# Gated mix of attention and MLP on one core: k and v summed in four column tiles, the gate's dot product on VectorE

## The chip, the cores and the metric

The kernel runs on one NeuronCore of one Trainium2 chip. The metric is the device time of one execution in microseconds (us); the time before is the median of three runs, 1220.77 us (1220.49 to 1221.15). PE is the matmul engine, PEld its weight loads, DVE the vector engine, ACT the scalar engine, POOL GpSimd, SP the queue from which most transfers are issued.

## The reference

One sequence of S = 2048 rows and width D = 512, all float32. An attention with 32 query heads of 16 elements and one shared key and value head, and an MLP with squared ReLU (width 1792), are mixed row by row with a scalar gate.

```python
def _A_ref(x, wq, wk, wv, wo):
    q = (x @ wq).reshape(B, S, H, Dh).transpose(0, 2, 1, 3)
    k = x @ wk
    v = x @ wv
    scores = jnp.einsum("bhqd,bkd->bhqk", q, k) * (Dh ** -0.5)
    p = _softmax(scores, axis=-1)
    o = jnp.einsum("bhqk,bkd->bhqd", p, v)
    return o.transpose(0, 2, 1, 3).reshape(B, S, H * Dh) @ wo

def _B_ref(x, w1, b1, w2, b2):
    h = jnp.maximum(jnp.einsum("bsd,df->bsf", x, w1) + b1, 0)
    return jnp.einsum("bsf,fd->bsd", h * h, w2) + b2

g = _sigmoid((x * gate_w).sum(-1, keepdims=True))
return g * _A_ref(x, wq, wk, wv, wo) + (1 - g) * _B_ref(x, w1, b1, w2, b2)
```

## The kernel before

**Two stages.** A short start, up to about 25 us, loads x, makes k and v for all 2048 rows and the first query tile, and sets up an upper bound of the scores. Then one long loop runs to the end. It goes over 32 query tiles (`it`: a column chunk `c` of 512 rows and a group of four heads), and for each over 32 units (128 keys by 256 queries by 4 heads). For every unit PE makes the scores (L757), ACT takes the exponential from PSUM to SBUF (L794), and PE sums e times v (L808, four heads in four column tiles of 32). Between the score matmuls of a unit, PE is given the matmuls of all other work (L1105): the remaining query tiles, the two MLP layers, the output projection. These stand in 64-row halves, so that each runs beside a score matmul of the other half. A unit of that other work is a *span*; `spans` counts them.

**What sets the order.** All instructions are issued by hand, engine by engine, in the order of the Python text (`manual_schedule`). In the loop a small planner decides: it keeps estimates of when PE, ACT and DVE are free (`at_pe`, `at_act`, `at_dve`), `PLANS` says where scores stand in a phase, and about a third of the score halves do not go straight to ACT: DVE copies them first (`score_copy`, L778, tile `x` to `e`), so that PSUM comes free earlier. DVE's other work waits in lists (`soon`, `divisions`, `chores`) with a price each; `spend` takes from them what, by these prices, fits ahead of such a copy, which may come `LATE` = 0.3 us after its scores. Entries of `chores` are strictly first in, first out; a load in that list returns how long its data is held back (`LANDS`, `DIVIDES`).

**The start.** `wkvf` holds wk, wv and gate_w as 33 used columns of 64, for four row tiles of D. For each chunk c of 512 rows, `kv_half` makes four float32 matmuls: row tiles 0 and 2 add up in the lower 64 partitions of a PSUM bank, 1 and 3 in the upper 64, in two column tiles. `kv_copy` (ACT) takes the bank to SBUF, `k_rows` (PE) adds the two halves and repeats k over the partitions with a constant matrix (`C_REP`), `k_square` and `k_round` (ACT) and `k_parts` (DVE) make k's two parts, and `k_norm` (a matmul on PE and a maximum on DVE) the largest norm of a key. After the four norms `km` and `k_shift` write a row of `k_aug`, without which no score can be made. `v_tiles` takes v and the gate's sum to rows with another constant matrix (`C_SEL`, 17 columns), `v_rows` copies them to `v_ext` and `z`, and `gate` (L518) turns z into g and 1 - g with two exponentials on ACT and four small operations on DVE; it is in the list `soon`. `wq_round` (ACT) and `wq_rest` (DVE) split the query weights into two float32r parts; `x_pair` and `x_split` do so for x.

**PSUM.** `kvp` are the two double banks that later hold scores (tile `s`); ks[0] and ks[1] are the banks of the first, ks[3] one bank of the second. Accesses of one double-bank tile are ordered as one tile: a write of one bank waits for the readers of the other that stand ahead of it.

Of the kernel before, what the change touches and what calls it, by code (L numbers as in the profile page):

```python
# [55 lines left out]
Q_ROWS = (0, 0, DH), (DH, 0, DH), (RS + 1, DH + 1, KS), (RS, DH, DH + 1)  # L56
LAST_OK = (NC * KT - 1) * len(PARTS)

C_ID, C_BLK, C_A, C_ONE, C_SEL, C_REP, C_N = 0, 128, 160, 161, 162, 179, 307


def constants():
    c = np.zeros((128, C_N), np.float32)
    c[:, :128] = np.eye(128)
    for p in range(128):
        c[p, C_BLK + p // 32 * 2 + p % 2] = 1.0
    for r in range(2):
        c[64 * r + 16:64 * r + 32, C_A] = -1.0
    c[:, C_ONE] = 1.0
    for a in (0, 64):  # L70
        for d in range(17):
# [89 lines left out]


@with_exitstack
def mix_kernel(ctx: ExitStack, tc: tile.TileContext, xT, wkv, wq, wo, w12, b1, b2, cst, out):
# [63 lines left out]
    with fast, tc.tile_pool(name="at", bufs=1) as at, \  # L228
# [18 lines left out]
        nc.sync.dma_start(wkvf, wkv)  # L247
        xf, xw = {}, {}

        def x_load(c):  # L250
# [32 lines left out]

        kvp = [sp.tile([128, 2, CH], F32, name="s") for _ in range(2)]
        ks = {0: kvp[0][:, 0], 1: kvp[0][:, 1], 3: kvp[1][:, 0]}
        sqk = at.tile([96, NC, CH], BF, name="sqk", tag="e", bufs=5)
        kvc = at.tile([128, NC, CH], F32, name="kvc", tag="e", bufs=5)
        kvq, kb = {}, {}

        def kv_half(c, a):  # L290

            if a == 0:
                kvq[c] = mp.tile([128, CH], F32, name="mm")
            for i in range(2):
                k = 2 * a + i
                nc.tensor.matmul(kvq[c][64 * i:64 * i + 64], wkvf[:, k], xf[c, k], start=a == 0, stop=a == 1,  # L296
                                 skip_group_check=True, tile_position=(0, 64 * i))

        def kv_copy(c):
            nc.scalar.activation(kvc[:, c], kvq[c], AF.Copy)  # L300

        def k_rows(c):

            if c == 2:
                ks[c] = mp.tile([128, CH], F32, name="mm")
            nc.tensor.matmul(ks[c], cs[:, C_REP:C_REP + 128], kvc[:, c], start=True, stop=True)  # L306

        def k_square(c):
            nc.scalar.activation(sqk[:, c], ks[c][:96], AF.Square)

        def k_round(c):
            kb[c] = of_tile("kb")
            nc.scalar.activation(kb[c], ks[c], AF.Copy)

        def k_norm(c):
            pn = kvp[0][:, 0] if c > 1 else mp.tile([128, CH], F32, name="mm")
            nc.tensor.matmul(pn, ones, sqk[:, c], start=True, stop=True)
            return lambda: nc.vector.tensor_reduce(kmx[:, c:c + 1], pn, AX.X, OP.max)

# [12 lines left out]
        def v_tiles(tiles, vp, idle=0):  # L332

            for i in tiles:
                c, j = divmod(i, 4)
                nc.tensor.matmul(vp[:, i * 17:i * 17 + 17], kvc[:, c, j * 128:(j + 1) * 128],
                                 cs[:, C_SEL:C_SEL + 17], start=True, stop=True)
# [174 lines left out]
        def wq_round(t):  # L512
            nc.scalar.activation(wqr[:, t], wqf[:, t], AF.Copy)

        def wq_rest(t):
            nc.vector.tensor_tensor(wql[:, t], wqf[:, t], wqr[:, t].bitcast(F32), OP.subtract)

        def gate():  # L518
            for o, s in ((g, -1.0), (omg, 1.0)):
# [20 lines left out]
        kv_half(0, 1)  # L540
        kv_copy(0)
        x_pair(0, 1)
# [12 lines left out]
        k_round(0)  # L555
        norm = k_norm(0)
        x_pair(1, 1)
        norm()
        kv_copy(1)
        kv_half(2, 0)  # L560
        kv_half(2, 1)
        k_rows(1)
        kv_copy(2)
        qnorm([(0, sq8[:, 0])], bank())
        k_square(1)
        k_round(1)
        k_parts(0)
        kv_half(3, 0)
        kv_half(3, 1)
        k_parts(1)  # L570
        kv_copy(3)
        wq_round(1)
        wq_rest(1)
        k_rows(2)
        norm = k_norm(1)
        norm()
        k_square(2)
        k_round(2)
        k_rows(3)
# [7 lines left out]
        k_round(3)  # L587
# [14 lines left out]
        chores, divisions = [], []  # L602
        soon = [(0, 0.7, lambda: wq_rest(3)), (1, 0.9, lambda: k_shift(2)), (2, 0.9, lambda: k_shift(3)),
                (2, 0.0, lambda: (w_load(0), w_load(1))), (2, 0.7, lambda: (act(0.64), wq_round(0), wq_rest(0)))]
        soon += [(5, 0.0, lambda: (w_load(0), w_load(1)))]
        soon += [(6, 1.2, lambda k=k: x_split(2, k)) for k in range(KT)]
        soon += [(10, 1.2, lambda k=k: x_split(3, k)) for k in range(KT)] + [(14, 2.0, gate)]
        ring, h, b2t, x, osp = [], [], [], dict(enumerate(zip(xr, xl))), {}

        def later(f, *args):  # L610
            chores.append((1.2, lambda: f(*args)))

        def have(half, n):
            while n not in ws[half]:
# [60 lines left out]
        def summed(c, fs, hs):  # L675

            n0 = c * NF
            if fs[0] == 0:
                res[c] = keep.tile(sh, F32, name=f"res{c}", tag="r0")
            have(1, n0 + fs[-1])  # L680
            for j in range(4):
                s, cols = 4 * c + j, slice(j * 128, (j + 1) * 128)
                part = res[c][:, j]
                if fs[0] == 0:
                    nc.gpsimd.tensor_scalar(part, b2t[0], omg[:, s:s + 1], None, op0=OP.mult)

                def done(p, s=s, part=part, j=j):
                    nc.vector.scalar_tensor_tensor(part, p, omg[:, s:s + 1], part, op0=OP.mult, op1=OP.add)
# [595 lines left out]
```

## Time and profile before

The profiled execution took 1220.05 us by its own time, 0.72 us below the median of the three runs; its span (first to last instruction) is 1218.3 us.

| what | value |
|---|---|
| PE | busy 1205.0 us, 99% of the span |
| ACT | busy 1035.9 us, 85% |
| DVE | busy 773.3 us, 63% |
| POOL | busy 64.6 us, 5% |
| first score matmul | at 25.15 us |
| first matmul on e and v | at 35.95 us |
| HBM read | 57.83 MB |

A busy PE is a PE that has a matmul in its pipeline; the chain that ended last says what the end waited for. A row of the timeline gives the start, the length until the last of its instructions ended, engine, source line, operation, operands, the count, and in brackets how long the engine had been idle and what ended that.

### The profile page before, as it was taken

Reading aid. Unit: us, or ns where it says so; the run is one execution under the profiler, and the core shown is the slowest. Engines: PE = TensorE matmul, PEld = TensorE weight load, DVE = VectorE, ACT = ScalarE, POOL = GpSimd, SP = SyncE. Lnnn points to the kernel's source line nnn. Section 1 sums busy time; section 2 is a strip of 40 time slices with the busy share of each in tenths; the row PEclk is TensorE's granted clock in tenths of the full one; section 3 lists DMA queues with packets and bytes.
Section 4 is the critical chain, followed back from the end, with each engine's and each line's share of the span. In section 5 each row is a group of like instructions: output and inputs, shape, how many; then the busy total and the mean of one; then the engine's idle time right before and its main releaser. Section 6 shows DMA issues by size and latency. Waiting matters only on the chain.

```text
span 1218.3 us, 24126 instructions
## 1 busy us (share of the span) xinstructions
PE 1205.0 (99%) x9846; PEld 669.3 (55%) x9846; DVE 773.3 (63%) x1514; ACT 1035.9 (85%) x1148; POOL 64.6 (5%) x87
## 2 busy tenths in 40 slices
PE   9999999999999999999999999999999999999997
PEld 4555555556555555555555555555555555555544
DVE  6865778576765855747758564755647586474543
ACT  6788888888888888888988888889988888888875
POOL 1000020000002000000002000000020000000000
PEclk9999999999999999999999999999999999999999
DMA  7344432121212222101314212121121222201101
GB/s 229 80 115 113 99 93 75 40 75 57 74 62 101 75 84 92 49 27 58 100 49 138 69 55 84 40 66 49 61 74 58 75 75 67 72 21 49 57 18 38
DMA packets 45347, 88.71 MB, mean 73 GB/s; under 512 B 10642, under 2 KB 10898, under 8 KB 44720
## 3 DMA queue, kind: packets, MB, share of 16 engines
q1 hardware_dynamic: 37024, 68.27, 18.3%
q0 software_dynamic: 8064, 18.59, 5.0%
q8 instruction: 79, 1.29, 0.4%
q14 instruction: 36, 0.29, 0.1%
q10 hardware_dynamic: 144, 0.26, 0.1%
HBM read 57.83 MB, written 20.97 MB: 65 GB/s over the span
## 4 chain that ended last, share of the span: by engine, by line
PE 92%; ACT 4%; DVE 2%; DMA 1%; issue 1%; SPq 0%; ACTq 0%; DVEq 0%
PE acc L808 36%; PE mm L1105 33%; PE s L757 17%; PE x L757 6%; ACT e L794 3%; DVE e L778 1%; PE mm L296 0%; DMA xf<-in_xT 0%; PE mm L200 0%; ACT w1r L497 0%; DMA w1f<-in_w 0%; DVE qr L392 0%; DVE ql L393 0%; DVE hr L192 0%; PE s L306 0%
## 5 line engine op out<-in xcount | busy, mean ns | idle before, releaser
L794 ACT ACTIVATE e<-s 128x1024 f32<-128x1024 f32 x822 | 781.5, 1026 | 158.5 <-PE s L757 156.9
L778 DVE COPY e<-x 128x512 f32<-128x512 f32 x404 | 278.9, 690 | 381.3 <-PE x L757 339.0
L808 PE MATMUL acc<-e,v_ext 128*32 128x512 f32 (+1 forms) x4224 | 482.7, 584 | 0.0
L757 PE MATMUL s<-qa,k_aug 49*128 49x512 f32 x1644 | 459.6, 412 | 0.1
L757 PEld LDWEIGHTS s<-qa,k_aug 49*128 49x128 f32 x1644 | 233.2, 185 | 77.4 <-ACT e L794 54.6
L808 PEld LDWEIGHTS acc<-e,v_ext 128*32 128x32 f32 x4224 | 116.3, 109 | 241.1 <-issue 237.4
L794 ACT ACTIVATE e<-e 128x1024 f32<-128x1024 f32 x202 | 214.5, 1062 | 0.8 <-DVE e L778 0.8
L1105 PE MATMUL mm<-w2r,hr 64*128 64x512 f32 x752 | 172.0, 403 | 0.0
L757 PE MATMUL x<-qa,k_aug 49*128 49x512 f32 x404 | 164.5, 407 | 1.8 <-DVE o L884 0.9
L1105 PEld LDWEIGHTS mm<-w2r,hr 64*128 64x128 f32 x752 | 110.5, 186 | 42.7 <-DVE hr L193 7.5
L757 PEld LDWEIGHTS x<-qa,k_aug 49*128 49x128 f32 x404 | 75.1, 186 | 48.6 <-DVE w2l L492 10.1
L1105 PE MATMUL mm<-w2l,hr 64*128 64x512 f32 x376 | 90.0, 392 | 0.0
L1105 PE MATMUL mm<-xlagain,w1r 64*128 64x512 f32 x224 | 70.7, 390 | 0.0
L1105 PE MATMUL mm<-xragain,w1r 64*128 64x512 f32 x224 | 69.9, 417 | 0.5
L1105 PE MATMUL mm<-xl,w1r 64*128 64x512 f32 x224 | 70.1, 391 | 0.0
L1105 PE MATMUL mm<-xr,w1r 64*128 64x512 f32 x224 | 69.3, 416 | 0.2
L833 DVE RECIPROCAL n<-n 128x86 f32<-128x86 f32 x90 | 61.5, 683 | 1.9
L1105 PE MATMUL mm<-more 64*128 64x512 f32 x216 | 60.7, 394 | 0.0
L1105 PEld LDWEIGHTS mm<-w2l,hr 64*128 64x128 f32 x376 | 56.8, 186 | 3.9
L1105 PEld LDWEIGHTS mm<-xragain,w1r 64*128 64x128 f32 x224 | 37.6, 185 | 28.2 <-issue 7.5
L1105 PEld LDWEIGHTS mm<-xr,w1r 64*128 64x128 f32 x224 | 37.4, 185 | 26.8 <-DVE big L664 5.0
L1105 PE MATMUL mm<-xragain,w1l 64*128 64x512 f32 x224 | 50.8, 393 | 0.0
(169 smaller groups left out, 1256.8 us busy)
## 6 DMA issues: line engine op xcount, KB each, us to landing
stage<-in_w SPq DMA_DIRECT2D x56, 256.0 KB
qa<-qs SPq DMA_DIRECT2D x186, 64.0 KB
w1f<-in_w SPq DMA_DIRECT2D x28, 256.0 KB
w2f<-in_w SPq DMA_DIRECT2D x28, 256.0 KB
qs<-qr SPq DMA_DIRECT2D x16, 256.0 KB
ress<-res POOLq DMA_DIRECT2D x4, 1024.0 KB, 4.2
qs<-ql POOLq DMA_DIRECT2D x15, 256.0 KB, 8.4
oc<-accs SPq DMA_DIRECT2D x30, 128.0 KB
```

What stands on the lines that cost most here:

```text
L757: nc.tensor.matmul(dst.rearrange("p (a n) -> p a n", a=2), k_aug[rows, kt * 128:(kt + 1) * 128], qa[it][rows, :, q * HC:q * HC + HC], star ...
L778: nc.vector.tensor_copy(e_half(u)[:, 2 * r:2 * r + 2], x.rearrange("p (a n) -> p a n", a=2))
L794: nc.scalar.activation(e_half(u), src, AF.Exp, scale=SCALE)
L808: nc.tensor.matmul(acc[h * 32:(h + 1) * 32, cols], v_ext[:, kt], es[u // 2][:, h % 2 * 2 + h // 2, mine], start=(kt == 0), stop=(kt == NK ...
L833: return ((0.23, bound), (0.35, compare), (0.72, lambda: nc.vector.reciprocal(n[0], n[0])), (0.28, lambda: nc.vector.tensor_tensor(o[:, co ...
L1105: nc.tensor.matmul((self.before if r else self).bank, a[p], b[p], start=not r and i == 0, stop=r == 1 and i == len(self.terms[1]) - 1, ski ...
```

## The change

k and v are summed in four column tiles: `wkvf` has 32 columns (wk and wv alone), and row tile k of D goes into partitions 32k to 32k+31, each matmul with start and stop of its own. The constants `C_REP` and `C_SEL` add four groups where they added two. `wkvf` is loaded from ACT's queue, not SP's. Odd chunks use the third kind of bank (`aside`, tile `x`). The norms of chunks 0 and 3 are made in the free bank of the second double-bank tile (`norms`), and in the start the readers of a double-bank tile stand behind the writes of its other bank. The residues `wq_rest` of weight tiles 1 and 2 go from DVE to POOL, and `wq_round(3)` goes behind `k_shift` on ACT.

The gate no longer comes out of `wkvf`. x is passed a second time in row order (`xs`, 16 tiles of 128 by 512) and gate_w as a vector, which is loaded once into all partitions (`gwb`, in a buffer of tile `lc`). Sixteen DVE instructions (`gate_sum`) multiply a tile of x by it and add up each row into a column of `z`; two tiles share a load (`gate_load`, 512 KB). They are entries of `chores`, priced 0.7 us each, the last one 2.7 us with `gate` behind it. `gate` is taken out of `soon`.

```diff
-C_ID, C_BLK, C_A, C_ONE, C_SEL, C_REP, C_N = 0, 128, 160, 161, 162, 179, 307
+C_ID, C_BLK, C_A, C_ONE, C_SEL, C_REP, C_N = 0, 128, 160, 161, 162, 178, 306
...
-        wkvf = at.tile([128, KT, 64], F32, name="wkvf", tag="w1f")
-        nc.sync.dma_start(wkvf, wkv)
+        wkvf = at.tile([128, KT, 32], F32, name="wkvf", tag="w1f")
+        nc.scalar.dma_start(wkvf, wkv)
...
+        gwb = at.tile([128, D], F32, name="gwb", tag="lc", bufs=2)
...
+        norms = kvp[1][:, 1]
...
-        def kv_half(c, a):
-            if a == 0:
-                kvq[c] = mp.tile([128, CH], F32, name="mm")
-            for i in range(2):
-                k = 2 * a + i
-                nc.tensor.matmul(kvq[c][64 * i:64 * i + 64], wkvf[:, k], xf[c, k], start=a == 0, stop=a == 1,
-                                 skip_group_check=True, tile_position=(0, 64 * i))
+        def kv_sums(c, parts=range(KT)):
+            if parts[0] == 0:
+                kvq[c] = aside() if c % 2 else mp.tile([128, CH], F32, name="mm")
+            for k in parts:
+                nc.tensor.matmul(kvq[c][32 * k:32 * k + 32], wkvf[:, k], xf[c, k], start=True, stop=True,
+                                 skip_group_check=True, tile_position=(0, 32 * k))
...
-            pn = kvp[0][:, 0] if c > 1 else mp.tile([128, CH], F32, name="mm")
+            pn = kvp[0][:, 0] if c == 2 else mp.tile([128, CH], F32, name="mm") if c == 1 else norms
...
-            vz = vp[:, :16 * 17].rearrange("p (i d) -> p i d", i=16)
-            nc.vector.tensor_copy(v_ext[:, :, 0:32:2], vz[:, :, :DH])
-            nc.vector.tensor_copy(z, vz[:, :, DH])
+            nc.vector.tensor_copy(v_ext[:, :, 0:32:2], vp[:, :NK * DH].rearrange("p (i d) -> p i d", i=NK))
...
-        kv_half(0, 0)
+        kv_sums(0, (0, 1))
         x_pair(0, 0)
-        kv_half(0, 1)
-        kv_copy(0)
+        kv_sums(0, (2, 3))
         x_pair(0, 1)
+        kv_copy(0)
...
+        x_pair(1, 0)
+        kv_sums(1)
         k_rows(0)
-        x_pair(1, 0)
+        x_pair(1, 1)
...
-        kv_half(1, 0)
-        kv_half(1, 1)
+        kv_copy(1)
+        kv_sums(2)
         k_square(0)
         k_round(0)
+        kv_copy(2)
+        k_rows(1)
+        k_parts(0)
         norm = k_norm(0)
...
         wq_round(1)
-        wq_rest(1)
+        wq_rest(1, nc.gpsimd)
...
         k_square(3)
+        k_round(3)
...
-        for t in (2, 3):
-            wq_round(t)
+        wq_round(2)
...
-        wq_rest(2)
+        wq_rest(2, nc.gpsimd)
...
-        soon = [(0, 0.7, lambda: wq_rest(3)), (1, 0.9, lambda: k_shift(2)), (2, 0.9, lambda: k_shift(3)),
+        soon = [(0, 0.7, lambda: (act(0.64), wq_round(3), wq_rest(3))), (1, 0.9, lambda: k_shift(2)), (2, 0.9, lambda: k_shift(3)),
...
-        soon += [(5, 0.0, lambda: (w_load(0), w_load(1)))]
+        soon += [(5, 0.0, lambda: (w_load(0), w_load(1), gates()))]
...
-        soon += [(10, 1.2, lambda k=k: x_split(3, k)) for k in range(KT)] + [(14, 2.0, gate)]
+        soon += [(10, 1.2, lambda k=k: x_split(3, k)) for k in range(KT)]
...
+        def gate_load(i):
+            if i == 0:
+                nc.sync.dma_start(gwb, bass.AP(tensor=gw.tensor, offset=gw.offset, ap=[[0, 128], [1, D]]))
+            nc.sync.dma_start(stage()[:, :2], xs[i:i + 2].rearrange("t p d -> p t d"))
+            return DIVIDES
...
+        def gate_sum(i):
+            rows = stage()[:, i % 2]
+            nc.vector.scalar_tensor_tensor(rows, rows, 1.0, gwb, op0=OP.mult, op1=OP.mult, accum_out=z[:, i:i + 1])
+            if i == NS - 1:
+                gate()
+                summed_gates.append(True)
+
+        def gates():
+            for i in range(NS):
+                if i % 2 == 0:
+                    chores.append((0.0, lambda i=i: gate_load(i)))
+                chores.append((0.7 if i < NS - 1 else 2.7, lambda i=i: gate_sum(i)))
```

**PE in the start.** `xf` and `xk` are chunks of x, `kvc` the copied sums, `sqk` the squares of k, `ones` and `blk` constants. Before, from the first sums of k and v to those of the last chunk:

```order
L296 MATMUL mm<-xf,wkvf 64x512 x4
L200 MATMUL mm<-xf,wqf 128x512 x4
L306 MATMUL s<-kvc,cs 128x512
L296 MATMUL mm<-xf,wkvf 64x512 x4
L317 LDWEIGHTS ones
L317 MATMUL mm<-sqk,ones 128x512
L296 MATMUL mm<-xk,wkvf 64x512 x4
L306 MATMUL s<-kvc,cs 128x512
L411 LDWEIGHTS blk
L411 MATMUL mm<-sq_142,blk 32x512
L296 MATMUL mm<-xk,wkvf 64x512 x4
```

And in the changed kernel:

```order
L297 MATMUL mm<-xf,wkvf 32x512 x4
L200 MATMUL mm<-xf,wqf 128x512 x4
L297 MATMUL x<-xf,wkvf 32x512 x4
L307 MATMUL s<-kvc,cs 128x512
L297 MATMUL mm<-xk,wkvf 32x512 x4
L307 MATMUL s<-kvc,cs 128x512
L318 LDWEIGHTS ones
L318 MATMUL s<-sqk,ones 128x512
L410 LDWEIGHTS blk
L410 MATMUL mm<-sq_143,blk 32x512
L297 MATMUL x<-xk,wkvf 32x512 x4
```

The sums of chunk 1 have moved ahead of the first `k_rows`, and the first norm behind the second `k_rows`.

**ACT at the end of the start**, from the last copy of sums to the first exponentials. Before:

```order
L300 ACTIVATE kvc<-mm 128x512
L513 ACTIVATE wqr<-wqf 128x512
L309 ACTIVATE sqk<-mm 96x512
L313 ACTIVATE kb<-mm 128x512
L309 ACTIVATE sqk<-s 96x512
L313 ACTIVATE kb<-s 128x512
L513 ACTIVATE wqr<-wqf 128x512 x2
L328 ACTIVATE k_aug<-km 1x512
L794 ACTIVATE e<-s 128x4x256 x4
```

And in the changed kernel:

```order
L301 ACTIVATE kvc<-x 128x512
L512 ACTIVATE wqr<-wqf 128x512
L310 ACTIVATE sqk<-mm 96x512
L314 ACTIVATE kb<-mm 128x512
L310 ACTIVATE sqk<-s 96x512
L314 ACTIVATE kb<-s 128x512
L512 ACTIVATE wqr<-wqf 128x512
L329 ACTIVATE k_aug<-km 1x512
L512 ACTIVATE wqr<-wqf 128x512
L813 ACTIVATE e<-s 128x4x256 x4
```

One of three roundings of wq has gone behind the shift row; the first still stands ahead of the squares of chunks 2 and 3.

**DVE where the last gate sum stands**, in the loop, behind one of the first units of the MLP (`big` and `hr` are its hidden values). Before:

```order
L778 COPY e<-x 128x2x256
L663 TENSOR_SCALAR big<-mm,b1t 128x512
L664 TENSOR_TENSOR big<-big 128x512
L192 CAST hr<-big 128x512
L193 TENSOR_TENSOR hr<-big,hr 128x512
L778 COPY e<-x 128x2x256 x2
```

And in the changed kernel, where ACT's two exponentials of the gate stand between `e<-e` and a run of five `e<-s` and wait for the sum:

```order
L797 COPY e<-x 128x2x256
L680 TENSOR_SCALAR big<-mm,b1t 128x512
L681 TENSOR_TENSOR big<-big 128x512
L192 CAST hr<-big 128x512
L193 TENSOR_TENSOR hr<-big,hr 128x512
L619 SCALAR_TENSOR_TENSOR stage,z<-stage,gwb 128x512
L520 TENSOR_SCALAR g<-g 128x16
L521 RECIPROCAL g<-g 128x16
L520 TENSOR_SCALAR omg<-omg 128x16
L521 RECIPROCAL omg<-omg 128x16
L797 COPY e<-x 128x2x256 x2
```

The sum and the gate have come in ahead of two copies; the other fifteen sums stand likewise, most of them ahead of one copy. Where the splits of wo stood among these places, they have gone later. PE's order in the loop is the same before and after.

More of the change, by code (lines that the diff above doesn't have):

```diff
@@ L69, in constants @@
     c[:, C_ONE] = 1.0
-    for a in (0, 64):
-        for d in range(17):
+    for a in range(0, 128, 32):
+        for d in range(DH):
             c[a + 16 + d, C_SEL + d] = 1.0
@@ L163, in mix_kernel @@
 @with_exitstack
-def mix_kernel(ctx: ExitStack, tc: tile.TileContext, xT, wkv, wq, wo, w12, b1, b2, cst, out):
+def mix_kernel(ctx: ExitStack, tc: tile.TileContext, xT, xs, gw, wkv, wq, wo, w12, b1, b2, cst, out):
     nc = tc.nc
@@ L335, in v_tiles @@
                 c, j = divmod(i, 4)
-                nc.tensor.matmul(vp[:, i * 17:i * 17 + 17], kvc[:, c, j * 128:(j + 1) * 128],
-                                 cs[:, C_SEL:C_SEL + 17], start=True, stop=True)
+                nc.tensor.matmul(vp[:, i * DH:i * DH + DH], kvc[:, c, j * 128:(j + 1) * 128],
+                                 cs[:, C_SEL:C_SEL + DH], start=True, stop=True)
                 for _ in range(idle):
@@ L513, in wq_round, with wq_rest @@
             nc.scalar.activation(wqr[:, t], wqf[:, t], AF.Copy)
-        def wq_rest(t):
-            nc.vector.tensor_tensor(wql[:, t], wqf[:, t], wqr[:, t].bitcast(F32), OP.subtract)
+        def wq_rest(t, eng=nc.vector):
+            eng.tensor_tensor(wql[:, t], wqf[:, t], wqr[:, t].bitcast(F32), OP.subtract)
         def gate():
@@ L551, in mix_kernel @@
         q_direct(RS + 1, ql, DH, (nc.sync, nc.gpsimd))
-        kv_half(1, 0)
-        kv_half(1, 1)
+        kv_copy(1)
+        kv_sums(2)
         k_square(0)
         k_round(0)
+        kv_copy(2)
+        k_rows(1)
+        k_parts(0)
         norm = k_norm(0)
[L557 to L564, printed above, removed]
+        qnorm([(0, sq8[:, 0])], mp.tile([128, CH], F32, name="mm"))
         k_square(1)
         k_round(1)
[L567 to L570, printed above, removed]
+        kv_sums(3)
+        norm()
         kv_copy(3)
         wq_round(1)
-        wq_rest(1)
+        wq_rest(1, nc.gpsimd)
+        norm = k_norm(1)
         k_rows(2)
-        norm = k_norm(1)
+        k_parts(1)
         norm()
+        k_rows(3)
         k_square(2)
         k_round(2)
-        k_rows(3)
         norm = k_norm(2)
@@ L586, in mix_kernel @@
         norm()
-        k_round(3)
-        for t in (2, 3):
-            wq_round(t)
+        wq_round(2)
         nc.vector.tensor_reduce(km, kmx, AX.X, OP.max)
@@ L683, in summed @@
                 part = res[c][:, j]
+                while not summed_gates:
+                    chores.pop(0)[1]()
                 if fs[0] == 0:
@@ L1265 @@
         "xT": c(np.asarray(inputs["A_x"])[0].reshape(NC, CH, KT, 128).transpose(0, 2, 3, 1)),
-        "wkv": c(np.concatenate([wk, wv, gw.reshape(D, 1), np.zeros((D, 31), np.float32)], axis=1)
-                 .reshape(KT, 128, 64).transpose(1, 0, 2)),
+        "xs": c(np.asarray(inputs["A_x"])[0].reshape(NS, 128, D)),
+        "gw": c(gw.reshape(D)),
+        "wkv": c(np.concatenate([wk, wv], axis=1).reshape(KT, 128, 32).transpose(1, 0, 2)),
         "wq": c(np.asarray(inputs["A_wq"]).reshape(KT, 128, KT, 2, 2, 2, DH).transpose(2, 1, 0, 3, 5, 6, 4)
```

3 lines of the change are left out of this document (2 added, 1 removed).

## The prediction

> **What bounds the kernel.** I read the page first: busy times, the slices with the granted clock, then the chain of work that ended last.
>
> ```profile
> PE 1205.0 (99%) x9846; PEld 669.3 (55%) x9846; DVE 773.3 (63%) x1514; ACT 1035.9 (85%) x1148; POOL 64.6 (5%) x87
> ...
> PEclk9999999999999999999999999999999999999999
> ...
> PE 92%; ACT 4%; DVE 2%; DMA 1%; issue 1%; SPq 0%; ACTq 0%; DVEq 0%
> ```
>
> PE carries 92% of the chain. In the loop PE's order does not change, so the change can act in three ways: the start can end earlier, a wait of PE can go, a wait can come. Next the timeline of the start:
>
> ```profile
> 0.74 0.40 SPq L247 DMA_DIRECT2D wkvf<-in_wkv  x1
> 1.19 3.69 PE L526 MATMUL acc<-wu 128*128 128x512 bf16 x10 [1.19 <-DVE wu L234]
> 1.20 0.93 SPq L255 DMA_DIRECT2D xf<-in_xT  x2
> 5.17 1.08 PE L296 MATMUL mm<-xf,wkvf 128*64 128x512 f32 x4 [0.29 <-DMA xf<-in_xT]
> 6.50 1.08 PE L296 MATMUL mm<-xf,wkvf 128*64 128x512 f32 x4 [0.25 <-DMA xf<-in_xT]
> 10.98 0.38 SPq L264 DMA_DIRECT2D wqf<-in_wq  x1
> 12.00 1.94 PE L296 MATMUL mm<-xf,wkvf 128*64 128x512 f32 x8
> 14.66 1.94 PE L296 MATMUL mm<-xk,wkvf 128*64 128x512 f32 x8 [0.40 <-ACT kvc L300]
> 17.90 1.94 PE L296 MATMUL mm<-xk,wkvf 128*64 128x512 f32 x8
> 20.41 0.62 ACT L513 ACTIVATE wqr<-wqf 128x512 fp32r<-128x512 f32 x1
> 20.93 0.59 ACT L309 ACTIVATE sqk<-mm 96x512 bf16<-96x512 f32 x1
> 22.50 0.59 ACT L313 ACTIVATE kb<-s 128x512 fp32r<-128x512 f32 x1
> 23.00 0.39 PE L317 MATMUL s<-sqk,ones 96*128 96x512 bf16 x1
> 23.43 0.69 DVE L318 TENSOR_REDUCE kmx<-s 128x1 f32<-128x512 f32 x1 [0.49 <-PE s L317]
> 24.54 0.42 DVE L330 TENSOR_SCALAR k_aug<-km 1x512 fp32r<-1x512 f32 x1
> 25.15 0.39 PE L757 MATMUL x<-qa,k_aug 49*128 49x512 f32 x1
> ```
>
> The chunks' sums take PE 1.08 us for a half chunk and 1.94 for a whole one. The last norm (23.43) opens the way to the shift row (24.54) and that to the first score (25.15). How fast x and wq come in is read from the same microseconds as windows; the last column is GB/s:
>
> ```profile
> 15.00:16.00 1.00, 1.00 (x6) 0.29 (x4) 0.98 (x2) 0.00 (x0) 0.05 (x1) 1.00 1.06 389
> 18.00:19.00 1.00, 1.00 (x6) 0.39 (x8) 0.95 (x2) 0.77 (x2) 0.00 (x0) 1.00 1.07 158
> 19.00:20.00 1.00, 1.00 (x5) 0.23 (x2) 1.00 (x3) 0.09 (x1) 0.57 (x2) 1.00 0.26 35
> ```
>
> The queue runs full until about 16 us and is empty just after 19. What SP issued last of the big loads, at 10.98 us, are tiles 1 to 3 of wqf. So they land near 19.1 us, an estimate from these rows (18.0 if the last microsecond belongs to small transfers of the query tile). ACT comes to them at 20.41: before, this load has 1.3 us to spare.
>
> **The start, step by step.** *Loads:* with wkvf off its queue SP issues x at 0.74 in place of 1.20, 0.46 us earlier, and wkvf is 64 KB smaller, 0.17 us at 389 GB/s. All later loads come between 0 (wkvf still in the way, on ACT's queue) and 0.63 us earlier. I take 0.5, nearer the top, since the queue is full from the first x on.
>
> *Sums:* that four column tiles of 32 run beside each other the loop shows:
>
> ```profile
> 35.95 2.78 PE L808 MATMUL acc<-e,v_ext 128*32 128x512 f32 x24
> ```
>
> 24 float32 passes in 2.78 us are 0.116 each; the 8 passes of a chunk in two tiles, 1.94, are 0.24 each. Chunk 0 stays, because its halves wait for x and have two tiles each as before. Chunks 1, 2 and 3 go from 1.94 to about 1.08 (a half chunk's time, with four tiles in place of two): 3 x 0.86 = 2.6 us less on PE. With PE's first matmul 0.3 earlier (the warm-up matmuls end at 4.88, so not the whole 0.5), PE would bring ACT to wqr 2.9 us earlier, at 17.5.
>
> *What is late next:* there the load is not yet in. ACT stands still until it lands, at 19.1 - 0.5 = 18.6, and the squares of chunks 2 and 3 stand behind wqr in ACT's queue, the last two norms on PE behind those. So ACT starts wqr at about 18.65 in place of 20.41, 1.76 earlier, and PE idles some 1.7 us.
>
> *From there:* wqr, square, copy, square, copy follow without another wait; from 20.41 to the end of the last copy, 22.50 + 0.59, it was 2.68 us, and without waits about 2.6: 21.25. New is that the last norm goes into the second bank of the tile which that copy reads, so it waits for the copy, where before it waited for the maximum ahead of it. 0.05 + 0.39 + 0.05 for it on PE, and the reduction starts at 21.75 in place of 23.43. The rest is as before, 1.72 us to the first score: 23.5, a gain of 1.7 us. DVE has a residue of wq (0.69) and the copy of z less behind that, which may add 0 to 0.4 before the first contexts; I take 0.1. **Start: -1.8 us** (-1.2 to -2.4 with the load at its ends).
>
> *On POOL* the residues of wq tiles 1 and 2 have no row. The nearest:
>
> ```profile
> L685 POOL TENSOR_SCALAR res<-big,omg 128x512 f32<-128x512 f32 x16 | 25.5, 1601 | 10.2 <-DMA ress<-res 9.0 <-ACT e L794 1.2
> 37.77 0.90 POOL L355 DMA_DIRECT2D qs<-ql  x1 [17.39 <-DVE ql L393]
> ```
>
> 1.6 us with one input tile; PE wants the first residue about 1 us after the first score, at 24.5, and it can start at 19.2. It would have to take over 5 us to cost anything; I cost it at 0, and at three times the row it still fits. POOL's next issue is 17 us away. The third rounding of wq, now behind the shift row on ACT (0.62), ends when the first scores do: 0.
>
> **The loop.** *The gate leaves its old place:*
>
> ```profile
> 67.05 0.21 ACT L520 ACTIVATE g<-z 128x16 f32<-128x16 f32 x1
> 67.29 0.18 DVE L521 TENSOR_SCALAR g<-g 128x16 f32<-128x16 f32 x1 [3.52 <-ACT g L520]
> 67.82 0.25 DVE L522 RECIPROCAL omg<-omg 128x16 f32<-128x16 f32 x1
> 69.99 0.50 PE L1105 MATMUL mm<-xr,wqr 64*128 64x512 f32 x2 [0.51 <-DVE ql L393]
> ```
>
> DVE is held 0.8 us, and at 69.99 PE waits 0.51 us for DVE. **-0.5 us** (0 to -0.8).
>
> *Sixteen sums* have no row with two SBUF inputs and an accumulator at this size. The nearest rows, and what DVE has left:
>
> ```profile
> L688 DVE SCALAR_TENSOR_TENSOR res<-mm,omg,res 128x512 f32<-128x512 f32 x64 | 47.5, 741 | 0.2 <-PE s L757 0.2
> L664 DVE TENSOR_TENSOR big<-big 128x512 f32<-128x512 f32 x56 | 38.9, 694 | 1.9
> L830 DVE DVE_READ_ACCUMULATOR lc<-n,lc 128x1 f32 x90 | 7.4, 83 | 0.0
> L778 DVE COPY e<-x 128x512 f32<-128x512 f32 x56 | 38.6, 689 | 36.0 <-PE x L757 28.6 <-PE mm L1105 3.6 <-PE s L757 3.3
> PE mm L1105 <- DVE ql L393: 0.7, 2, 0.5
> 109.00:146.00 37.00, 36.79 (x308) 19.85 (x306) 28.80 (x63) 30.69 (x34) 4.01 (x6) 1.00 0.36 92
> ```
>
> 694 + 83 to 741 + 83 ns: 0.78 to 0.82 us, 0.1 over the planner's price. Together 12.8 us between about 40 and 187 us, where DVE waits 36 us ahead of the copies, 0.64 per copy, and PE waits for DVE 0.7 us at L1105. In the window where DVE is fullest, 28.8 of 37 us, 3 us more still fit. Cost 0; without that cover up to 0.1 a sum, 1.6. The splits of wo give up places there and go later. The loads, 16 tiles of 256 KB and gwb, are 4.4 MB over 150 us, 30 GB/s on top of 92; behind them in SP's queue stand query tiles that are due a whole tile (37 us) later. 0.
>
> *The last sum* is not hidden. Where it will stand:
>
> ```profile
> 186.02 0.69 DVE L193 TENSOR_TENSOR hr<-big,hr 128x512 fp32r<-128x512 f32 x1
> 186.62 4.77 ACT L794 ACTIVATE e<-s 128x1024 f32<-128x1024 f32 x5 [0.82 <-PE s L757]
> ```
>
> The sum follows the split, 186.71 to 187.5, then ACT's two gate exponentials, which stand ahead of these five, 0.15 later, with 0.1 to the next start. So the five start 1.1 us later than at 186.62; they run without a gap, so what is lost comes back to PE through the score banks. The DVE copy behind the gate slips 1.6 us, but its exponential is the sixth, 4.5 us off. **+1.0 us** (+0.3, if PE's lead takes most of it, to +2.5, with DVE's 1.6 us on top).
>
> **Sum:** -1.8 - 0.5 + 1.0 = -1.3 us. Against the profiled execution's 1220.05 (span 1218.3) that is 1218.75; the runs' median, 1220.77, lies 0.72 higher, so I forecast 1219.5 us.
>
> **Rivals.** *The load is not the end of the start.* If wqf's tiles land near 17.5, PE's 2.9 us count in full: 1.3 us more, 1218.2. For it: the rate falls from 389 before the end, so others share the tail. Against: 768 KB after eight tiles of x cannot be through much sooner.
>
> *The sums hold up the copies* (the other side). A sum stands directly ahead of a copy; a copy may be 0.3 us late by the planner. At 1.3 us a sum, 0.6 over its price, 0.3 would show each time: 16 x 0.3 = 4.8 us, and 1224.3. Slower from 1.23 us a sum on. For it: no row has this form in place. Against: 741 and 83 ns, and 0.64 us of idle time per copy.
>
> *The last sum costs its upper end*, 2.5: 1221.0, nothing won.
>
> [...]
>
> *The four tiles run one after another*, so the change does not do what it says: 8 x 0.43 = 3.4 us a chunk (a pass alone, from 1.94 for four rounds), 1.5 more than before in three chunks. 4.5 us later less the 0.3 of the earlier first matmul, -0.5 + 1.0 + 4.2 = +4.7: 1225.5. Against: the L808 row.
>
> **How the numbers follow.** Forecast 0.57 (own range 1218.2 to 1220.8), earlier load 0.15, sums 0.10, last sum 0.12, clock 0.03, tiles 0.03. A measurement of this kernel tells about 0.2%, 2.4 us, from no change: the bounds are 1218.3 and 1223.2. Faster: 0.15 and 0.06 of the forecast's own low end, 0.21. Slower: 0.10 + 0.03, 0.13. The same: 0.66. The range, 1217.4 to 1222.3, leaves out the sums, the tiles, the clock and a few hundredths below.
>
> **What would show it.** In the changed profile: a chunk's sums x8 at about 1.1 us; ACT idle until wqf lands, then wqr at 18 to 19 us; the first score near 23.5, first contexts near 34.1; no PE wait near 68 us; sums of 0.78 to 0.82 us, with no PE wait for DVE beside them; ACT idle for its gate exponential near 185 us and PE idle about 1 us after it. I am wrong if wqr starts at 17.5, if a sum takes over 1 us, or if PE waits at more than one of the sixteen places.

## The result, and the profile after

The changed kernel takes 1226.86 us (median of five runs, 1226.74 to 1227.31), the kernel before 1220.77 us on the same chip: a ratio of 1.0042, with a 95% interval of 1.003 to 1.0054. It is 6.1 us slower, where 1.3 us less were forecast. The profiled execution took 1226.76 us, its span is 1224.9.

On the changed kernel's page the busy times hardly differ from before, and the chain is PE's as before. One line differs:

```profile
PE 1210.1 (99%) x9846; PEld 674.8 (55%) x9846; DVE 781.7 (64%) x1543; ACT 1036.8 (85%) x1148; POOL 68.0 (6%) x89
...
PEclk8899999999999999999999999999999999999999
...
PE 92%; ACT 3%; DVE 2%; DMA 1%; issue 0%; SPq 0%; DVEq 0%; ACTq 0%
```

In the first two of the 40 slices, the first 61 us, TensorE was not granted its full clock. Windows of a microsecond show where it changes. The number behind POOL's is the granted clock, the last two are the DMA share and GB/s:

```profile
22.00:23.00 1.00, 1.00 (x12) 0.97 (x12) 0.64 (x1) 0.42 (x1) 0.51 (x1) 1.00 0.34 25
23.00:24.00 1.00, 1.00 (x10) 0.80 (x8) 0.90 (x4) 0.53 (x1) 0.76 (x1) 0.69 0.52 174
24.00:25.00 1.00, 1.00 (x4) 0.78 (x5) 0.97 (x3) 0.72 (x2) 0.00 (x0) 0.50 0.69 199
...
39.00:40.00 1.00, 1.00 (x8) 0.78 (x6) 0.11 (x1) 0.23 (x2) 0.00 (x0) 0.50 0.98 336
40.00:41.00 1.00, 1.00 (x10) 0.81 (x8) 0.00 (x0) 0.80 (x1) 0.00 (x0) 0.78 0.87 236
```

The clock halves inside the microsecond from 23 and is full again in the one from 40. The trace's own records of the clock put it at 23.38 to 40.44 us, 17.07 us at half rate. The timeline of that start:

```profile
5.08 1.06 ACT L530 ACTIVATE xr<-xf 128x1024 fp32r<-128x1024 f32 x1 [2.60 <-DMA xf<-in_xT]
11.12 0.38 SPq L264 DMA_DIRECT2D wqf<-in_wq  x1
11.14 1.07 PE L297 MATMUL x<-xf,wkvf 128*32 128x512 f32 x8
13.19 1.06 PE L297 MATMUL mm<-xk,wkvf 128*32 128x512 f32 x8
18.12 1.10 PE L307 MATMUL s<-kvc,cs 128*128 128x512 f32 x2
19.34 0.63 ACT L512 ACTIVATE wqr<-wqf 128x512 fp32r<-128x512 f32 x1 [1.40 <-DMA wqf<-in_wq]
20.50 0.38 PE L318 MATMUL s<-sqk,ones 96*128 96x512 bf16 x1 [1.28 <-ACT sqk L310]
20.71 0.29 PE L337 MATMUL acc<-cs,kvc 128*128 128x16 f32 x2
20.85 0.26 PE L340 MATMUL acc<-sqk,ones 96*128 96x240 bf16 x1
21.95 0.38 PE L318 MATMUL s<-sqk,ones 96*128 96x512 bf16 x1 [0.34 <-ACT kb L314]
24.60 0.62 PE L776 MATMUL x<-qa,k_aug 49*128 49x512 f32 x1
26.31 0.62 PE L1124 MATMUL mm<-xr,wql 64*128 64x512 f32 x1
26.74 0.62 PE L1124 MATMUL mm<-xr,wqr 64*128 64x512 f32 x1
```

The sums of a chunk take the forecast 1.07 us. ACT then stands still until wq lands, PE behind it, and from 20.50 us on PE has, beside the last two norms, small matmuls only (two of 16 columns and one of 240 at a time). The first score comes at 24.60, in place of 25.15 before, but at half clock: the 64-row matmuls of the loop start 0.43 us apart, against 0.23 in the kernel before:

```profile
26.24 0.39 PE L1105 MATMUL mm<-xr,wql 64*128 64x512 f32 x1
26.48 0.39 PE L1105 MATMUL mm<-xr,wqr 64*128 64x512 f32 x1
```

The start of each exponential that reads PSUM, compared in the two traces, shows where the time went. PE's order in the loop is the same, so the n-th of one kernel answers to the n-th of the other:

| place | before | after | difference |
|---|---|---|---|
| first exponential | 26.03 | 25.76 | -0.27 |
| ninth, the clock full again | 35.53 | 41.04 | +5.5 |
| behind the gate's old place | 86.27 | 90.80 | +4.5 |
| ahead of the last gate sum | 182.01 | 186.62 | +4.6 |
| behind it | 186.62 | 192.15 | +5.5 |
| last exponential | 1205.48 | 1211.12 | +5.6 |

Before the ninth exponential 5.8 us are lost; all that the change does in the 1170 us behind it adds up to 0.1. (From the last exponential's end to the span's end it is 11.8 us in before's profile and 12.7 in this one; DVE's last instruction ends 7.1 us behind that exponential in both, so this difference lies behind the work of the engines.)

### The profile page after: what moved, and what is told of

It is laid out like the page before. It is cut to its first block, busy times and chain, and to the rows that moved or that the text cites. A ratio compares the mean times of both kernels' runs of the same rounds, so it can differ in the third digit from the quotient of the medians.

```text
span 1224.9 us, 24165 instructions
## 1 busy us (share of the span) xinstructions
PE 1210.1 (99%) x9846; PEld 674.8 (55%) x9846; DVE 781.7 (64%) x1543; ACT 1036.8 (85%) x1148; POOL 68.0 (6%) x89
## 4 chain that ended last, share of the span: by engine, by line
PE 92%; ACT 3%; DVE 2%; DMA 1%; issue 0%; SPq 0%; DVEq 0%; ACTq 0%
PE acc L827 36%; PE mm L1124 33%; PE s L776 17%; PE x L776 6%; ACT e L813 2%; DMA wqf<-in_wq 1%; DMA xk<-in_xT 1%; DVE e L797 0%; ACT w1r L496 0%; PE acc L337 0%; DMA w1f<-in_w 0%; DVE hr L192 0%; PE acc L340 0%; SPq L255 0%; DVE big L681 0%
```

## Experiments

The first theory is that the clock fell because TensorE had too little to do, the rivals that the gate on VectorE holds the loop up or that the start is late for another reason. The granted clock of each run tells at once whether it fell at the start: its mean is 0.996 to 0.999 where it did not, 0.989 to 0.994 where it did.

**Six matmuls in PE's wait.**

```diff
         k_rows(3)
+        for _ in range(6):
+            nc.tensor.matmul(pw, wu[:, :128], wu, start=True, stop=True)
         k_square(2)
```

> The changed kernel with six more matmuls of 128 by 128 by 512 in bfloat16 (the warm-up's operands, into the accumulator bank, read by nobody) on PE behind the last k_rows, where PE idles from 19.22 to 20.50 us for ACT. Theory A (the TensorE clock halves because the array has too little to do between 19.2 and 23.4 us, and that costs all of the loss): no record of half clock in the loop, first score at about 24.1 us, and -1.0 (first score before: 25.15) - 0.55 (old gate place) + 0.3 (fifteen sums) + 0.9 (last sum) = about 1220.4 us (1219.8 to 1221.3). Rival B (sums, loads and the gate on VectorE hold up the loop; the clock is a side show): 1226.3 to 1227. Rival C (what counts is the stretch of small matmuls from 20.5 us on, not the idle time ahead of it): the clock still falls, 1226 to 1227.

Measured: median 1220.82 us of 12 runs, before 1221.25 (ratio 1.0002, 0.9984 to 1.0019). In two of the 12 runs the clock fell all the same (1227.3 and 1227.7); the other ten took 1219.6 to 1222.3. The profiled one:

```profile
18.87 1.46 PE L575 MATMUL acc<-wu 128*128 128x512 bf16 x6
...
24.09 0.49 PE L778 MATMUL x<-qa,k_aug 49*128 49x512 f32 x1
```

```profile
19.00:20.00 1.00, 1.00 (x7) 0.43 (x5) 0.05 (x1) 0.67 (x2) 0.00 (x0) 1.00 0.13 24
...
24.00:25.00 1.00, 0.90 (x5) 0.54 (x5) 0.97 (x3) 0.72 (x2) 0.00 (x0) 1.00 0.63 166
```

Nobody reads these six matmuls and they shorten nothing, yet the kernel is 6 us faster (1220.82 against 1226.86). With the clock held, the exponentials start 1.1 us earlier than before at 49 us and 0.7 earlier at the end. So the gate is not the loss (rival B). That it can still fall says that what stands behind the wait counts too (part of rival C).

**The same six, a sixteenth of the array.** Same places and lengths, but 32 rows by 32 columns:

```diff
+            nc.tensor.matmul(pw[:32], wu[:32, :32], wu[:32], start=True, stop=True)
```

> The run with six fillers in PE's wait at 19.22 us, but each filler 32 rows by 32 columns in place of 128 by 128: as many, as long (512 columns), a sixteenth of the array. Array theory (the clock follows the share of the array's cells at work, rows times columns times time, over records of 3.413 us): the fillers add next to nothing, the clock falls in all or nearly all runs, 1226.2 to 1228.6 us. Time theory (it follows whether PE streams at all): as with the full fillers, the clock falls in 2 of 12 runs, the others 1219.6 to 1222.3 us.

Measured: median 1226.96 us; the clock fell in 9 of 12 runs (1226.7 to 1229.5), the other three took 1219.8 to 1221.5. In its profile:

```profile
18.86 1.46 PE L575 MATMUL acc<-wu 32*32 32x512 bf16 x6
```

```profile
19.00:20.00 1.00, 1.00 (x6) 0.37 (x4) 0.00 (x0) 0.71 (x2) 0.00 (x1) 1.00 0.19 37
...
25.00:26.00 1.00, 1.00 (x6) 0.80 (x4) 1.00 (x3) 0.68 (x1) 0.00 (x0) 0.50 0.64 227
```

PE is as busy from 19 to 20 us as with the full fillers (1.00 of 1.00 us in both), and the clock falls in 9 runs of 12 in place of 2. The fillers of the two kernels differ in their rows and columns alone, 32 by 32 against 128 by 128; PE's busy time does not tell these kernels apart. The expectation "nearly all" was a little too strong.

**The kernel before, without its own filler.** Nothing of the change is in it; the nine matmuls L339 of the start are left out, whose result nobody reads:

```diff
-        v_tiles(range(3), vp, 1)
+        v_tiles(range(3), vp)
...
-        v_tiles(range(3, 9), vp, 1)
+        v_tiles(range(3, 9), vp)
```

> The kernel before, without the nine matmuls of 96 by 128 by 240 that stand between the first v tiles in the start and whose result nobody reads. Nothing of the change is in it. Array theory: the least share over a record's length falls from about 0.38 to about 0.2, so the clock falls at the start in most runs, and these take 1226 to 1229 us; the others 1219.8 to 1223. Rival (the clock's fall belongs to the wait for wq's load or to the four column tiles, which this kernel has not): all runs 1219.5 to 1223 us, as before.

Measured: median 1225.47 us; the clock fell in 10 of 12 runs (1225.2 to 1227.0), the other two took 1219.5 and 1221.0. Its profile has the clock at half rate in the loop:

```profile
27.00:28.00 1.00, 1.00 (x5) 0.91 (x4) 1.00 (x3) 1.00 (x2) 0.00 (x0) 0.50 0.26 102
```

The loss of the changed kernel can be had without the change. So neither the four column tiles nor the wait for wq is needed for it.

**No square behind the load.** The first rounding of wq goes behind the last copy of k on ACT:

```diff
         kv_copy(3)
-        wq_round(1)
-        wq_rest(1, nc.gpsimd)
...
         k_round(3)
+        wq_round(1)
+        wq_rest(1, nc.gpsimd)
```

> The changed kernel with the first rounding of wq behind the copy of k of the last chunk on ACT, so that no square stands behind the load of wq. Theory A: squares start at about 18.3 instead of 19.87, PE does not idle at 19.2, the last norm comes at about 20.7 instead of 21.95, and the first score at 22.7 to 23.1 instead of 24.60. If the clock holds: about 1220.8 - 2.2 - 0.55 + 0.3 + 0.9 = 1219.2 us (1218.5 to 1219.8). Rival C (the small matmuls alone drop the clock, with or without the wait): half clock in the loop, 1224.5 to 1226. Rival D (the late load is not what ACT waits for): first score where it is, 1226.9.

Measured: median 1223.18 us of 12 runs: six with the clock fallen (1225.6 to 1227.1) and six without (1218.5 to 1220.7). The first score came at 22.45 us, earlier than expected, and of the runs that kept the clock two lie where theory A put them (to 0.1 us) and four up to 0.9 us above. Half the runs fall as rival C has it. The wait is gone and the small matmuls are left.

**Rounding late and full fillers.** With that, the v tiles' own filler is made 128 by 128 by 256 (for the seven tiles inside the loop too), and two stand behind each of the first six tiles:

```diff
-                    nc.tensor.matmul(vp[:, 272:], ones, sqk[:, 0, 272:], start=True, stop=True)
+                    nc.tensor.matmul(vp[:, 256:], wu[:, :128], wu[:, :256], start=True, stop=True)
...
-        v_tiles(range(3), vp, 1)
+        v_tiles(range(3), vp, 2)
...
-        v_tiles(range(3, 9), vp, 1)
+        v_tiles(range(3, 6), vp, 2)
+        v_tiles(range(6, 9), vp, 1)
```

> The changed kernel with the first rounding of wq behind the last copy of k on ACT, and with full fillers (128 by 128 by 256) in place of the nine 96 by 128 by 240, two for each of the first six v tiles and one for the next three. Array theory: the least share is 0.43 or more up to the first score, so the clock holds in all runs or all but one; first score at 22.5 to 22.9; 1218.5 to 1221 us, median 1219.6. Rival (the loop's own first microseconds, of a share of 0.40 to 0.45, are as dangerous): falls in a quarter or more of the runs.

Measured: median 1219.52 us (1217.4 to 1219.9, 11 runs, none with the clock fallen), before 1221.98: a ratio of 0.9973 (0.9958 to 0.9988). This beats both kernels. Its start:

```profile
20.25 1.15 ACT L512 ACTIVATE wqr<-wqf 128x512 fp32r<-128x512 f32 x2
20.42 0.38 PE L318 MATMUL s<-sqk,ones 96*128 96x512 bf16 x1
20.83 0.69 DVE L319 TENSOR_REDUCE kmx<-s 128x1 f32<-128x512 f32 x1 [0.64 <-PE s L318]
22.88 0.39 PE L777 MATMUL x<-qa,k_aug 49*128 49x512 f32 x1
```

**The kernel before with the same fillers** tells how much of this the clock alone gives.

```diff
-                    nc.tensor.matmul(vp[:, 272:], ones, sqk[:, 0, 272:], start=True, stop=True)
+                    nc.tensor.matmul(vp[:, 272:], wu[:, :128], wu[:, :240], start=True, stop=True)
```

(and the counts as above)

> The kernel before, with the full fillers in place of the 96 by 128 by 240 ones, as many and at the same places as in the run with the late rounding and the full fillers. Array theory: the least share rises from 0.38 to about 0.48, no run falls (before: 7 of 58 did), 1219.8 to 1223 us, and the runs of before that did not fall are not beaten: so what the changed kernel with a mended start gains on before (2.5 us) comes from the change, but for 0.3 to 0.5. Rival (the whole gain is the clock's): this kernel is as fast as that one, 2.5 us below before.

Measured: median 1222.28 us (1220.7 to 1223.3, 12 runs, none fallen), before 1222.14, ratio 0.9999 (0.9989 to 1.0009). So the fillers alone give nothing that can be told here, and the 2.5 us of the run above come from the change with the rounding late: the earlier first score, 22.88 in place of 25.15, is nearly all of it. The late rounding alone was not tried in the kernel before, so its share in the 2.5 us is not shown.

**The changed kernel again.** No edit.

> The changed kernel as it is, in more runs, since only five were there and the record's phase differs from run to run. Array theory: the least share is below 0.33 for every phase (records that begin from 18.2 to 21.5 us), so every run falls at the start: 1226.2 to 1229 us. Rival (it depends on the phase, as in the other kernels): one run in six or more at 1220 to 1223 us.

Measured: median 1227.49 us (1226.0 to 1229.0); the clock fell in all seven runs, as in the five of the result and the five of the first try under "The last sum", whose start is the same. Of the kernel before, 9 of the 82 runs made beside these experiments fell (1225.4 to 1229.0).

**Only the gate moved**, in the kernel before (its start and its 64 columns kept).

> The kernel before, with only the gate moved to VectorE (16 sums, their loads, gate behind the last); the start, with two column tiles and 64 columns of wkvf, as before (the gate's column is still summed there, but read by nobody). Theory A: clock full in the loop, 1220.8 - 0.55 + 0.3 + 0.9 = 1221.4 us (1220.9 to 1222). Rival B (the gate's sums and loads are the loss): 1226 to 1227.

Measured: median 1221.78 us (1220.8 to 1223.6, 11 runs, none fallen), before 1221.25, ratio 1.0 (0.9992 to 1.0009). The gate on VectorE costs nothing that can be told from no change, and rival B is out.

**The last sum.** The first try gave the gate's six instructions an entry of their own.

```diff
-            if i == NS - 1:
-                gate()
-                summed_gates.append(True)
...
+            chores.append((2.0, lambda: (gate(), summed_gates.append(True))))
```

> The changed kernel with the gate's own six instructions as a chore of their own behind the sixteenth sum (0.7 and 2.0 in place of one entry of 2.7), so that ACT's two exponentials need not wait for the sum. The start is untouched, so the clock falls as in the changed kernel. Last-sum theory (ACT's wait for the sum costs the 0.9 us by which the loop slips at 187 us): 1226.9 - 0.9 = 1226.0 us. Rival (DVE's time is what is lost there, and it is lost wherever the gate stands): 1226.6 to 1227.

Measured: median 1228.42 us (1226.2 to 1228.6), the clock fallen in all five, and ACT waits 1.51 us for the sum at the same place as in the changed kernel. The edit did not do what it was meant to: the sum and the gate stand there because the second layer's first part needs `omg` and takes whatever of `chores` is left, with any price. To get them out, the loads' allowance has to fall. In the run with late rounding and full fillers:

```diff
-            return DIVIDES
+            return LANDS
...
-            if i == NS - 1:
-                gate()
-                summed_gates.append(True)
+            return 1.5 if i == NS - 1 else None
...
-                chores.append((0.7 if i < NS - 1 else 2.7, lambda i=i: gate_sum(i)))
+                chores.append((0.7, lambda i=i: gate_sum(i)))
+            chores.append((1.0, lambda: (gate(), summed_gates.append(True))[1]))
```

> The run before, and the gate out of its forced place: the sums' loads are given 6 in place of 10 us, the gate's own instructions are a chore of their own priced 1.0, 1.5 us behind the last sum. By the order they then stand some 20 us earlier, with all sums done. Last-sum theory (the 0.9 us at 187 us is ACT's wait for a sum that is forced there because the second layer needs the gate): no ACT wait for the sum, 0.9 us less than the run before, median 1218.7 us. Rival (DVE's time is what is lost): the same as the run before.

Measured: median 1227.9 us (1224.0 to 1229.5, 6 runs). Rows of its waits from 100 to 128 us (in total, times, longest) and of its timeline:

```profile
DVE stage L620 <- DMA stage<-in_xs: 11.3, 2, 10.2
...
PE x L776 <- DVE e L797: 8.6, 1, 8.6
```

```profile
107.26 5.81 SPq L431 DMA_DIRECT2D qa<-qs  x8
113.17 0.39 SPq L613 DMA_DIRECT2D stage<-in_xs  x1
```

A sum waited 10.2 us for its load, which stood in SP's queue behind eight query loads that took 5.8 us to issue; a copy stood behind the sum on DVE, and PE waited 8.6 us for that copy. This is the mechanism of "the sums hold up the copies", by another door: not the sum's length but its load. The clock fell there as well. PE had no matmul from 114.0 to 122.57 us, and the clock was at half rate from 118.96 to 125.79 (PE's busy time comes first in the row, the clock stands third from its end):

```profile
119.00:120.00 1.00, 0.00 (x0) 0.00 (x0) 0.00 (x0) 0.00 (x0) 0.00 (x0) 0.50 0.42 150
```

With 9 us:

> The run with the late rounding and the full fillers, and the gate out of its forced place: the sums' loads are given 9 in place of 10 us (6 was too little: a sum waited 10.2 us for its load), the gate's own instructions are a chore of their own priced 1.0, behind the last sum. By the order ACT's two exponentials then stand one run of three exponentials earlier than the second layer's first use, with all sums done. Last-sum theory: ACT does not wait for a sum near 184 us, the loop does not slip 0.7 there, median about 0.8 us below the run with the fillers alone (1219.5 against 1222.0 of before), so 3.3 us below before. Rival 1 (DVE's time is what is lost there): 2.5 below before, as with the fillers alone. Rival 2 (9 us is too little as well): a sum waits for its load somewhere, 1219.5 or more.

Measured: median 1219.77 us (1217.9 to 1223.5, 12 runs, none fallen), before 1222.14, ratio 0.9982 (0.9968 to 0.9996). No slip is left where the sum was, but one of 0.7 us stands one exponential ahead of it:

```profile
DVE g L520 <- ACT g L519: 1.3, 1, 1.3
DVE stage L620 <- DMA stage<-in_xs: 1.1, 1, 1.1
```

Now DVE waits 1.3 us for ACT's exponential, and behind the place the exponentials are 0.2 us earlier than in the run with the fillers alone (0.1 earlier ahead of it already), at the end 0.04 later. So in these two profiles the move gains 0.1 us at most, not the 0.8 of the last-sum theory. The times themselves do not tell the two apart: the interval reaches from 0.5 to 3.9 us below before and holds both 2.5 and 3.3. That DVE's time is the cause (rival 1) is not shown, since this run has waits of its own.

## Why the prediction was wrong

**The step that failed** is that the forecast's sum, -1.8 - 0.5 + 1.0, takes the clock as held while PE waits. The chance of 0.03 for a fall rests on no run: none shows that a wait of this length is safe, and the runs showed the opposite. PE waited 1.28 us, less than the forecast's 1.7, and the clock fell in 12 runs of 12. That should have been the forecast.

Two readings were at fault. First, the wait was priced alone, where by the estimate below the work of the microseconds behind it counts as well. The trace's own records of the clock give stretches of 17.07 us at half rate and 1181.01 at full rate in the changed kernel's profile, and one of 1211.73 at full rate in before's: 5, 346 and 355 times 3.413 us. The stretches of 13.65 (narrow fillers), 6.83 (late rounding, full fillers and the gate apart) and 3.41 us (only the gate moved, near the end) at half rate are four, two and one of that length. A stretch of 3.413 us, counted from the first rise in a profile, is called a record here; the fall at 23.38 stands at the end of the record from 19.96 to 23.38. What the array does in it can be added up from rows. A 512-column bf16 matmul takes 0.216 us at full clock (the six fillers above: 1.46 less the 0.38 of one, over five steps), and a plain float32 record of 512 columns twice that (the L200 of before's start stand 0.43 us apart at 8.04, 8.47 and 8.90 us). So there are two norms of 96 rows, 2 x 0.216 x 96/128 = 0.32; eight L340 of 240 columns, 8 x 0.1 x 96/128 = 0.6; and sixteen plain float32 records of 16 columns, 16 x 0.0135 = 0.2. Together 1.1 us of full array in 3.41, a share of 0.33. The idle 0.54 us at its head are only a part of what is missing. The same sum for all records at full clock in the profiles of the start gives the table, whose shares are estimates from each run's matmul rows; the least share is over a stretch of 3.41 us wherever it begins, 15 to 34 us:

| kernel | record ahead of the fall, or the lowest that held | least share | runs fallen |
|---|---|---|---|
| changed kernel | 0.33 and 0.25 fell | 0.22 | 12 of 12 |
| the same, gate's instructions apart | 0.22 fell | 0.19 | 5 of 5 |
| before, filler left out | 0.29 fell | 0.17 | 10 of 12 |
| narrow fillers | 0.33 fell | 0.21 | 9 of 12 |
| late rounding | 0.38 fell | 0.33 | 6 of 12 |
| six full fillers | 0.39 held | 0.30 | 2 of 12 |
| gate only | 0.40 held | 0.36 | 0 of 11 |
| before | 0.45 held | 0.38 | 9 of 82 |
| before, full fillers | 0.51 held | 0.46 | 0 of 12 |
| late rounding, full fillers | 0.51 held | 0.48 | 0 of 11 |

Of the records in the table every one that fell has 0.38 or less, every one that held 0.39 or more; the two lie side by side. The records begin at another time in each profile (the clock first rose at 3.98 us in before's, 6.31 in the changed kernel's, 4.05 with the narrow fillers). That this is why a kernel with a least share near 0.38 fell in a part of its runs is the author's estimate and was not shown. The order within the table is not perfect (the six fillers fell less often than the late rounding), and why is open. That the measure is rows times columns times time is an estimate too; in the profiles of before and of the changed kernel it fits over their whole length. Summed so for every record at full clock from the first rise on, the 703 that held have 0.45 or more, the one at 19.96 us, which fell, 0.33, and the two ahead of the falls at 1215.71 and 1221.45 us, where the kernels run out of matmuls, 0.26 and 0.21.

Second, a window's granted clock of 1.00 says nothing of the microseconds ahead of the trace's first record of the clock. That record begins at 3.98 us in before's profile and at 6.31 in the changed kernel's, and the window 3.00:4.00 of the changed kernel reads 1.00 while its warm-up matmuls start 0.43 us apart, twice the 0.216 of full clock. The row of before could have told it: ten of them in 3.69 us are 0.37 each.

**What the fall cost.** The clock stayed down for five records, 17.07 us, and PE lost 6.4 us of its lead (in the run with six fillers the ninth exponential stands 0.9 us ahead of before's, here 5.5 behind). The loop's first work is 64-row matmuls, one at a time: four records with shares of 0.45 to 0.63 at half clock (the same sum, each matmul counted at twice its time) were followed by another at half rate, one of 0.94, when pairs of matmuls ran, by the rise at 40.44 us.

**Point by point:**

- *Sums of k and v:* 1.06 and 1.07 us where 1.08 was forecast, for two of the three whole chunks (1.24 for the third). Right.
- *Loads 0.5 us earlier:* wrong. SP issued the rest of wq at 11.12 us (10.98 before), ACT had the first of x at 5.08 (5.06 before), and wqr started at 19.34, not 18.65. The 0.46 us that SP won at the head did not last. PE's first sums, forecast 0.3 us earlier, came 0.4 later (5.57, before 5.17): the clock first rose at 6.31 us, not 3.98. In the run with the narrow fillers it rose at 4.05, and they came at 4.91.
- *What is late next:* right in kind. ACT waited 1.40 us for wq, PE 1.28 for ACT. With the clock held the first score came at 24.09 us, 1.06 earlier than before; 1.7 was forecast, and the late load, 0.7, accounts for the difference. Before's start, though, does not always end at 25.15, which it did with the first rise of the clock at 3.98 us: in the run with only the gate moved, whose start is the same, the clock rose at 7.03 us and the first score came at 25.78. The changed start, which waits for wq, gave 24.04 and 24.09 with rises at 4.05 and 6.30. So what it gains differs from run to run, 1.1 to 1.7 us in these profiles.
- *Residues on POOL:* 1.27 us, under the 1.6 taken; nothing waits for them.
- *Old gate place:* -0.5 forecast; the difference falls by 0.6 from 63 to 71 us (5.46 to 4.88), and the 0.51 us that PE waited for DVE at 69.99 are gone. Right. From the ninth exponential to the one at 86 us it falls by 1.0 in all; the other 0.4 (at 49 and 86 us) were not forecast and are not explained, but stand in the run with only the gate moved as well.
- *Sixteen sums:* 0.68 and 0.08 us each, 0.76 where 0.78 to 0.82 was forecast; over the nine between 86 and 182 us the difference grows by 0.1.
- *Last sum:* +1.0 forecast, +0.9 measured, at the place and with the wait of ACT that was named (of PE's idle time of about 1 us, forecast behind it, a wait of 0.42 for ACT shows, at 193.20):

```profile
191.19 0.68 DVE L619 SCALAR_TENSOR_TENSOR stage<-stage,gwb 128x512 f32<-128x512 f32 x1
191.80 0.08 DVE L619 DVE_READ_ACCUMULATOR stage<-stage,gwb 128x1 f32 x1
191.92 0.22 ACT L519 ACTIVATE g<-z 128x16 f32<-128x16 f32 x1 [1.50 <-DVE stage L619]
192.15 4.66 ACT L813 ACTIVATE e<-s 128x1024 f32<-128x1024 f32 x5
```

With the clock held, the change as it stands (the six fillers) ended 0.7 us ahead of before by the last exponential, where 1.3 was forecast; the medians do not tell it from no change.

## What to carry to other kernels

When a change makes a start shorter by taking work from TensorE, add up what the array does over the next few microseconds, not only how long PE waits: here a start with a least share of 0.22 (estimated as above) fell in 12 runs of 12 and cost 6 us, and six useless matmuls in the wait gave them back in 10 runs of 12. Matmuls that look like waste may be what holds the clock: without the nine that nobody reads, the kernel before fell in 10 runs of 12, with them in 9 of 82. Before any are taken out or moved, count them. And compare several runs, since some of these kernels fell in some runs and not in others (the late rounding in 6 of 12).

## What was not expected of the hardware

- A share at which the clock held at full rate did not bring it back from half. In before's profile a record of 0.45 held; in the changed kernel's four records at half clock with 0.45 to 0.63 stayed there. The records ahead of the rises of these two profiles have 0.83 (at 3.98 us), 0.86 (6.31) and 0.94 (40.44). All are estimates, summed as above.
- Near the end of the kernel, where PE waits for ACT and DVE, one more record falls in some runs (in the run with the late rounding two) and rises again after 3.41 us. In the profile of the kernel with only the gate moved:

```profile
1181.00:1182.00 1.00, 1.00 (x10) 0.46 (x14) 0.65 (x2) 1.00 (x2) 0.00 (x0) 0.60 0.00 0
1182.00:1183.00 1.00, 1.00 (x16) 0.43 (x12) 0.00 (x0) 1.00 (x2) 0.00 (x0) 0.50 0.00 0
...
1185.00:1186.00 1.00, 1.00 (x9) 0.69 (x9) 0.33 (x1) 0.11 (x1) 0.00 (x0) 1.00 0.00 0
```

  It costs 1.6 us by the exponentials behind it. By the author's estimate it is what spreads the runs of the kernel before that did not fall at the start over 1219.8 to 1223.6 us: of these 73, the 33 with a mean granted clock of 0.999 have a median of 1220.7, the 40 with 0.997 or 0.998 one of 1222.2 (3.41 us at half rate take 0.0014 off the mean). A filler for that place was not tried.
